# A two-layer transformer kernel: its head rebuilt, the first block in halves, gate rows from column strips, and another order of work

## The chip, the cores and the metric

The kernel runs on one NeuronCore of one Trainium2 chip. The metric is the device time of one execution in microseconds (us); lower is better. Engines are named as the profile names them: PE (TensorE, matrix products), PEld (its weight loads), DVE (VectorE), ACT (ScalarE), POOL (GpSimd) and SP (SyncE, which only issues DMAs and semaphore waits here). A name with a q (SPq, ACTq) is that engine's sequencer issuing a DMA.

## The reference

Input x is 1 × 2048 × 448 in bf16. One condition vector c (1 × 448) gives six modulation rows. Layer A is causal attention with 16 heads of 28 and a window of 256; layer B is a gated MLP that mixes over the sequence.

```python
mod = silu(c) @ w_mod                       # 448 x (6 * 448): sa, ca, ga, sb, cb, gb
h = layernorm(x) * (1 + ca) + sa
q, k, v = split(h @ wqkv)                   # 16 heads of 28
p = softmax(where(0 <= i - j < 256, q k^T / sqrt(28), -1e9))
x = x + ga * ((p v) @ wo)
h = layernorm(x) * (1 + cb) + sb
z1, z2 = split(gelu(h @ w_in))              # 896 columns each
g = w_sp @ layernorm(z2) + b_sp             # over the 2048 rows
x = x + gb * ((z1 * g) @ w_out)
```

## The kernel before

The sequence is cut into 16 tiles of 128 rows (`t` or `j`), four tiles to a block (`tb`). For each block x is normalized (`xn`, tile statistics at L591, normalization at L604 on DVE or L610 on POOL), transposed to `hT` (features on partitions) and modulated with `modT`. Blocks 0 and 1 are transposed by PE (L660) and modulated as they are copied out of PSUM (L672, L674); blocks 2 and 3 by DMA transposes on SP, and then modulated in place (L655). Products with `WQK` (L689) give `qT` and `KT`, four groups of four heads each, and products with `wv` (L742) give `Vaug`, values with a column of ones. `WQK` is made from the staged `wq_st` by a copy that spreads heads of 28 columns over 32 (L583 on ACT, L584 on DVE or POOL).

For each tile j come scores (L818 for the first two tiles, L844 and L853 after them; L853 needs `QBD`, a block-diagonal copy of q which SP spreads by four small DMAs per block, L720), exp on ACT (L805), a mask product on DVE (L860, L880), the products with the values (L887), the division (L901, L903), a DMA transpose, and the output projection (L912) with `wo_g`, which is wo with its columns scaled by the gate `ga` (POOL, L580). Then come the second normalization, a second transposing, w_in products with gelu (L997, L1018), the mixing products (L1041) against the DMA-transposed w_sp (`wspA`, `wspB`), and the final products (L1058) whose sums with x (`fin`, L1068, DVE) SP writes out.

The modulation is made of `sc_sb` (silu of c, on partitions) and `wmod`. For the first layer 32 products of one column write `modT` columns (L528). For the second layer 40 more do (L528, L533), and each gate row is made on all 128 partitions by four products against `sc_rep`, c copied 128 times (L574), and copied to `gg_sb` (L577).

The program is recorded as operations with dependencies. The table `ORDER` lists them: each word has the number of an operation, its engine and its buffers, and every engine runs its operations in that order. `Sched.waits` adds the semaphore waits that the dependencies need, and only those. Durations and landing times in the code serve the making of the table; nothing is computed from them on the chip. PE also runs filling products on the identity matrix (L559), whose results nobody reads.

Loads are issued by SP and ACT. The load of `wv`, the second quarter of x and the rest of `wmod` wait on SP until the first part of `wmod` has landed; the third and fourth quarter of x stand on SP behind the spread of q for block 0.

## Time and profile before

| | us |
|---|---|
| median of 3 runs | 280.66 |
| the three runs | 280.28, 280.66, 281.29 |
| the profiled execution, first to last instruction | 281.0 |
| PE busy in it | 269.3 (96%) |
| DVE busy | 164.3 (58%) |
| ACT busy | 128.5 (46%) |
| POOL busy | 126.1 (45%) |

The profiled execution is one run of the program; its span lies among the times of the three runs. In a row of the windows the first column is the stretch in us from the span's start and its length; then come the busy us and the instruction count of each engine, the granted clock of PE (1.00 is full), the mean busy share of the 16 DMA engines, and GB/s. In a row of the timeline stand start and length in us, engine, line, operation, and in brackets the idle time before it and what ended it. In a row of the chain of waits stand start, length and what ran. A PE product's own length includes its way through the array; where many follow each other, the step from one row to the next tells what each costs.

### The profile page before, as it was taken

The page shows a single profiled execution, that of the slowest core. Times are in us where ns is not written, and L with a number is a line of the kernel's source. Part 1 is how long each engine was busy: PE and PEld are TensorE (multiplying, and loading weights), DVE is VectorE, ACT ScalarE, POOL GpSimd, SP SyncE. Part 2 cuts the span into 40 slices and gives each one's busy share as a digit, 9 for nine tenths or more (in the row PEclk, how much of TensorE's full clock was granted, in tenths as well). Part 3 has the DMA queues.
Part 4 walks back from the last instruction along what each step waited for, and adds up shares of the span by engine and source line. Part 5 has one row for each costly group of instructions (what it writes and reads, how often), then busy time and mean ns, then how long its engine had stood idle before and what let it go on. Part 6 is the DMA issues. An engine that isn't in the chain of part 4 may idle for free.

```text
span 281.0 us, 7380 instructions
## 1 busy us (share of the span) xinstructions
PE 269.3 (96%) x3198; PEld 142.3 (51%) x3222; DVE 164.3 (58%) x355; ACT 128.5 (46%) x151; POOL 126.1 (45%) x200
## 2 busy tenths in 40 slices
PE   6799999799999999999999999999999999999995
PEld 2445556456657777544444444444444444444452
DVE  6347999599899999968898600000243003124443
ACT  4548899789999999866666700000000000000000
POOL 8231177921027989947769503001477101436110
PEclk9789999999999999999999999999999999999999
DMA  6775735343315485693699989910000000000032
GB/s 199 188 261 157 267 58 98 84 55 72 72 23 75 63 96 80 162 103 79 125 181 186 168 181 201 163 36 0 0 2 0 0 0 2 16 16 16 19 98 98
DMA packets 65347, 26.01 MB, mean 93 GB/s; under 512 B 56418, under 2 KB 64227, under 8 KB 65315
## 3 DMA queue, kind: packets, MB, share of 16 engines
q1 hardware_dynamic: 64496, 24.39, 43.6%
q10 hardware_dynamic: 818, 1.15, 1.5%
q8 instruction: 25, 0.41, 0.6%
q14 instruction: 8, 0.06, 0.1%
HBM read 9.01 MB, written 1.84 MB: 39 GB/s over the span
## 4 chain that ended last, share of the span: by engine, by line
PE 80%; POOL 5%; DVE 4%; ACT 4%; issue 3%; DMA 3%; ACTq 0%; POOLq 0%
PE ps L1041 34%; PE ps L997 8%; PE ps L1058 8%; PE ps L1018 8%; PE ps L689 6%; PE ps L887 4%; ACT PW L805 3%; PE ps L912 3%; DMA wmod<-in_w_mod_dram 3%; PE ps L844 2%; PE ps L742 2%; PE ps L853 1%; POOL xn L610 1%; PE ps L729 1%; POOL wo_g L580 1%
## 5 line engine op out<-in xcount | busy, mean ns | idle before, releaser
L805 ACT ACTIVATE PW<-ps 128x2048 bf16<-128x2048 f32 (+1 forms) x56 | 67.8, 1240 | 4.3 <-PE ps L844 2.6
L1048 POOL TENSOR_TENSOR z1T<-tmpg,z1T 128x512 bf16<-128x512 bf16 x28 | 31.7, 1152 | 77.9 <-DVE tmpg L1045 77.9
L1045 DVE TENSOR_TENSOR tmpg<-ps,bsp_bc 128x512 bf16<-128x512 f32 x28 | 19.0, 689 | 79.2 <-PE ps L1041 70.3
L1041 PE MATMUL ps<-wspB,z 128*128 128x512 bf16 x219 | 49.2, 379 | 0.3
L1041 PE MATMUL ps<-wspA,z 128*128 128x512 bf16 x219 | 48.9, 379 | 0.4 <-issue 0.2
L860 DVE TENSOR_TENSOR PT<-PW,mask 128x1024 bf16<-128x1024 bf16 x56 | 39.2, 729 | 0.3 <-ACT PW L805 0.2
L1041 PEld LDWEIGHTS ps<-wspA,z 128*128 128x128 bf16 x224 | 21.8, 98 | 26.6 <-issue 0.4
L1041 PEld LDWEIGHTS ps<-wspB,z 128*128 128x128 bf16 x224 | 21.9, 98 | 26.3
L596 POOL TENSOR_SCALAR ve_all<-mv_all 128x1 f32<-128x1 f32 (+2 forms) x37 | 11.3, 312 | 46.7 <-DVE mv_all L594 45.9
L689 PE MATMUL ps<-hT,WQK 128*128 128x512 bf16 x98 | 25.5, 388 | 2.4 <-POOL hT L655 1.4
L597 POOL TENSOR_TENSOR rs_all<-ve_all,neghalf 128x1 f32<-128x1 f32 (+2 forms) x37 | 25.3, 694 | 1.1
L887 PE MATMUL ps<-Vaug,PT 128*128 128x32 bf16 x496 | 24.4, 177 | 0.5 <-DVE PT L860 0.5
L887 PEld LDWEIGHTS ps<-Vaug,PT 128*128 128x128 bf16 x496 | 21.8, 96 | 4.4 <-DVE o_sb L903 0.9
L997 PE MATMUL ps<-w_in,hT 64*128 64x448 bf16 x224 | 22.7, 349 | 0.2 <-ACT PW L805 0.2
L1018 PE MATMUL ps<-hT,w_in 64*128 64x512 bf16 x196 | 22.3, 376 | 0.0
L1058 PE MATMUL ps<-w_out_g,z1T 128*128 128x448 bf16 x112 | 21.8, 353 | 0.0
L887 PE MATMUL ps<-Vaug,PW 128*128 128x32 bf16 x224 | 20.2, 176 | 0.0
L591 DVE BATCH_NORM_STATS2 st_all<-x_sb 128x6 f32<-128x448 bf16 x32 | 19.2, 610 | 0.4 <-DMA x_sb<-in_A_x_dram 0.4
L610 POOL TENSOR_SCALAR xn<-x_sb,rs_all,ve_all 128x448 bf16<-128x448 bf16 x22 | 18.9, 863 | 0.3
L887 PEld LDWEIGHTS ps<-Vaug,PW 128*128 128x128 bf16 x224 | 17.6, 96 | 1.9
L591 DVE BATCH_NORM_STATS2 st_all<-z 128x6 f32<-128x448 bf16 x32 | 18.1, 602 | 0.2 <-ACT z L1004 0.2
L1004 ACT ACTIVATE z<-ps 128x896 bf16<-128x896 f32 x16 | 14.1, 915 | 8.3 <-PE ps L997 8.2
(100 smaller groups left out, 333.1 us busy)
## 6 DMA issues: line engine op xcount, KB each, us to landing
out_dram<-fin SPq DMA_DIRECT2D x16, 112.0 KB, 1.7
x_sb<-in_A_x_dram SPq DMA_DIRECT2D x3, 448.0 KB, 4.9
wmod<-in_w_mod_dram SPq DMA_DIRECT2D x1, 1344.0 KB, 8.6
w_in<-in_B_w_in_dram SPq DMA_DIRECT2D x1, 1344.0 KB, 8.9
QBD<-qT SPq DMA_DIRECT2D x16, 64.0 KB, 2.0
w_out_g<-in_B_w_out_dram SPq DMA_DIRECT2D x1, 784.0 KB, 5.3
bsp_bc<-in_B_b_sp_dram SPq DMA_DIRECT2D x1, 512.0 KB, 6.8
wmod<-in_w_mod_dram SPq DMA_DIRECT2D x2, 224.0 KB, 6.1
```

Source lines behind the costliest of these rows:

```text
L591: st = [dve(0.62 if True else 0, lambda e, t=t, ci=ci, s=s: e.bn_stats(st_all[:, slot, t, ci, :], s()), deps(t), prio) for ci, s in enumer ...
L597: rs = pool(0.53 + 0.15 * len(tiles), lambda e: e.tensor_tensor(rs_all[:, slot, a:b], ve_all[:, slot, a:b], neghalf[:, 0:b - a], ALU.pow), ...
L610: "pool": (0.9, lambda e: e.tensor_scalar(to[:, h.slot[0], 0:D], x_sb[:, t, :], z, ve, ALU.mult, ALU.add))}, [nm], prio, [h])
L689: mms = [lambda e, h=h, g=g, kc=kc, tb=tb: e.matmul(ps[:, h.slot[0], :], lhsT=WQK[:, kc, 4 * g:4 * g + 4, :].rearrange("p a b -> p (a b)") ...
L805: ex = act(xdur, lambda e, out_ap=out_ap, in_ap=in_ap: e.activation(out_ap(), in_ap(), ACT.Exp, scale=SCALE), [s], v - 8.0 + u, takes, tab ...
L860: return dve(0.70, lambda e: e.tensor_tensor(cols(hp.slot[0] * 2048 + 1024 * k, [[256, 4], [128, 2], [1, 128]]), cols(at_w() + 128 + 192 * ...
L887: fns.append(lambda e, hp=hp, hO=hO, hi=hi, bi=bi, kb=kb, hd=hd, nb=nb, a=at[hi][bi], p_of=p_of: e.matmul(ps[:, hO.slot[0], 32 * hd:32 * h ...
L997: return lambda e, kc, p0, start, stop: e.matmul(ps[:, hs[t % 2].slot[hf], 0:D], lhsT=hT[p0:p0 + 64, kc, t * 128:(t + 1) * 128], rhs=w_in[ ...
L1018: return lambda e, kc, p0, start, stop: e.matmul(ps[:, hs[b // 2].slot[b % 2], :], lhsT=w_in[p0:p0 + 64, kc, ft * 128:(ft + 1) * 128], rhs ...
L1041: m = pe(16 * MMS, [lambda e, h=h, si=si, ft=ft, tb=tb: e.matmul(ps[:, h.slot[0], :], lhsT=z2[:, si, ft * 128:(ft + 1) * 128], rhs=(wspA i ...
L1048: u = pool(1.16, lambda e, ht=ht, ft=ft, tb=tb: e.tensor_tensor(z1T[tb][:, ft, :], tmpg[:, ht.slot[0], :], z1T[tb][:, ft, :], ALU.mult), [ ...
L1058: return [lambda e, ft=ft: e.matmul(ps[:, h.slot[0], 0:D], lhsT=z1T[t // 4][:, ft, (t % 4) * 128:(t % 4 + 1) * 128], rhs=w_out_g[:, ft, :] ...
```

## The change

One line of loads. All loads of the head but that of c are now issued by SP, in the order of need and without waits: two tiles of x, the first 960 columns of w_mod in four pieces of rows, two tiles of x, the q and k columns of wqkv in four pieces, wv, the second quarter of x, the rest of w_mod, the third quarter, wo, the fourth quarter. On SP, before, in the order of the program (`wmod` here is w_mod in SBUF, `wq_st` the staged q and k weights):

```order
L415 DMA x_sb<-in_A_x_dram 128x2x448
L410 DMA wmod<-in_w_mod_dram 128x896
L411 DMA wmod<-in_w_mod_dram 64x896
L410 DMA wq_st<-in_A_wqkv_dram 128x896
L411 DMA wq_st<-in_A_wqkv_dram 64x896
L397 DMA wv<-in_A_wqkv_dram 128x3x448 [waits d_wmAb,d_wmAc,d_wmAa]
L398 DMA wv<-in_A_wqkv_dram 64x448
L404 DMA x_sb<-in_A_x_dram 128x4x448
L397 DMA wmod<-in_w_mod_dram 128x3x1792
L398 DMA wmod<-in_w_mod_dram 64x1792
L720 DMA QBD<-qT 32x2x512 [waits act]
```

and now, further down the same queue, from the second quarter of x on:

```order
L414 DMA x_sb<-in_A_x_dram 128x4x448
L409 DMA wmod<-in_w_mod_dram 128x3x1728
L410 DMA wmod<-in_w_mod_dram 64x1728
L414 DMA x_sb<-in_A_x_dram 128x4x448
L409 DMA wo_g<-in_A_wo_dram 128x3x448
L410 DMA wo_g<-in_A_wo_dram 64x448
L414 DMA x_sb<-in_A_x_dram 128x4x448
L562 DMA modrow<-rows_68 4x448 [waits act]
L564 DMA gg_sb<-modrow 128x448 [waits d_mr0]
L481 DMA_TRANSPOSE hT<-xn 128x4x128 [waits dve]
L481 DMA_TRANSPOSE hT<-xn 128x4x128 [waits pool]
```

The wait for the first part of w_mod is gone, the x quarters stand ahead of everything that waits for a computation, and the spread of q (L686 now) follows the four transposes of block 2.

First block in halves. Block 0 is normalized, transposed, modulated and projected as two halves of 256 rows, and the products of the first half are ordered by row pieces of the weights, as these become ready. The modulation of the first layer is added up over four groups of eight products, one group for each piece of w_mod, and one DVE reduction writes `modT`. On PE the stretch from the first transposes to the first dense products was (L660 transposes, L528 modulation, L559 filling, L689 projections):

```order
L660 MATMUL ps<-ident,xn 128x128 x4
L528 MATMUL ps<-sc_sb,wmod 128x1 x12
L528 MATMUL ps<-sc_sb,wmod 64x1 x4
L528 MATMUL ps<-sc_sb,wmod 128x1 x12
L528 MATMUL ps<-sc_sb,wmod 64x1 x4
L660 MATMUL ps<-ident,xn 128x128 x12
L559 MATMUL ps<-ident 128x512 x4
L689 MATMUL ps<-hT,WQK 128x512
L559 MATMUL ps<-ident 128x512 x2
L689 MATMUL ps<-hT,WQK 128x512 x23
```

and is now, around the second half's transposes (L627 transposes, L548 filling, L646 projections of a half, L672 values of block 0):

```order
L548 MATMUL ps<-ident 128x512
L548 MATMUL ps<-ident 128x128
L627 MATMUL ps<-ident,xn 128x128 x4
L548 MATMUL ps<-ident 128x128 x3
L627 MATMUL ps<-ident,xn 128x128 x4
L548 MATMUL ps<-ident 128x128 x2
L646 MATMUL ps<-hT,WQK 128x256
L548 MATMUL ps<-ident 128x512
L672 MATMUL ps<-wv,hT 128x448 x4
L646 MATMUL ps<-hT,WQK 128x256 x16
```

The modulation products now stand ahead of the transposes, the filling is spread among the products in pieces of 512 and 128 columns, and the projections go by 256 columns.

Gates as column strips. The four rows ga, gb, sb, cb are made at once on four strips of 32 output columns of the array (16 products of 448 columns), copied to `rows4`, written to DRAM, and read back: the gates broadcast to 128 partitions, the second layer's modulation gathered into `modT`. The one that is added to 1 gets it from a row of ones in `wmod`.

Also: the products with the values use 29 columns instead of 32, so that three columns of `Vaug` need no zeros; tile 1 is written out in two halves of columns, the second as the last of the program; some zeroing moves between engines; and of the 32 normalizations DVE now does 24 instead of 10. On DVE, before, from a normalization of block 1 to the third mask product (L880, L860 masks, L577 gate rows):

```order
L604 TENSOR_SCALAR xn<-x_sb,mv_all,rs_all 128x448 [waits pool]
L577 COPY gg_sb<-ps 128x448 [waits pe]
L880 TENSOR_TENSOR PT<-PT,mask_60 128x4x128 [waits act]
L604 TENSOR_SCALAR xn<-x_sb,mv_all,rs_all 128x448 [waits pool]
L880 TENSOR_TENSOR PT<-PT,mask_60 128x4x128
L577 COPY gg_sb<-ps 128x448 [waits pe]
L674 TENSOR_SCALAR hT<-ps,modT 128x512 [waits pe]
L674 TENSOR_SCALAR hT<-ps,modT 128x512 [waits dve]
L880 TENSOR_TENSOR PT<-PT,mask_60 128x4x128 [waits act]
```

and now, up to the second mask product (L578 statistics, L677 and L790 values to `Vaug`, L591 normalization, L903 masks):

```order
L730 TENSOR_SCALAR hT<-ps,modT 128x512 [waits act]
L578 BN_STATS st_all<-x_sb 128x6 [waits d_x3]
L677 CAST Vaug<-ps 128x16x28 [waits pe]
L591 TENSOR_SCALAR xn<-x_sb,mv_all,rs_all 128x448 [waits pool]
L578 BN_STATS st_all<-x_sb 128x6
L790 CAST Vaug<-ps 128x16x28 [waits pe]
L903 TENSOR_TENSOR PT<-PW,mask_60 128x1024
L591 TENSOR_SCALAR xn<-x_sb,mv_all,rs_all 128x448 [waits pool]
L903 TENSOR_TENSOR PT<-PW,mask_60 128x1024
```

The statistics of the third and fourth quarter of x, which wait for their loads, stand ahead of the first mask. Between the first and the last mask on DVE there are 14 statistics instead of 20, and 10 normalizations instead of 1.

The core of the diff (of the table `ORDER` one line of each):

```diff
-2.a 21.v 30.g 1.s 22.v 23.v 24.v 33.g 34.g 0.a 4.s 31.g 3.a 28.g 25.v 5.s 32.g 6.a 26.v 35.g 50.v 51.p.0 7.s 40.a 8.s 52.p.1 36.g 107.v 53.p.2 109.v
...
-    t_wmA = load3("d_wmA", wmod, w_mod, slice(0, 2 * D), -98.95, 7.75, 4.5, 6.7)
-    t_wq = load3("d_wq", wq_st, A_wqkv, slice(0, 2 * D), -98.9, 9.6, 8.4, 9.4)
-    t_wv = load2("d_wv", "sp", 0.35, wv, ALL, A_wqkv, slice(2 * D, 3 * D), [t_wmA], -95.5)
+    t_wmA = [chunk("d_wmA", "sp", wmod, w_mod, kc, slice(0, 2 * D + 64), -98.95 + 0.001 * kc, LAND_M[kc], 0.23) for kc in range(DC)]
+    t_x0.append(load("d_x01", "sp", 0.25, lambda e: e.dma_start(x_sb[:, 2:4, :], x_d[:, 2:4, :]), prio=-98.92, land=7.8))
+    t_wq = [chunk("d_wq", "sp", wq_st, A_wqkv, kc, slice(0, 2 * D), -98.9 + 0.001 * kc, LAND_Q[kc], 0.23) for kc in range(DC)]
+    t_wv = load2("d_wv", "sp", 0.35, wv, ALL, A_wqkv, slice(2 * D, 3 * D), (), -95.5)
...
+    t_rows = pe(0.8, [lambda e, v=v, i=i, kc=kc: e.matmul(
+        ps[32 * i:32 * i + 32, hR.slot[0], 0:D], lhsT=sc_rep[:, kc, :], rhs=wmod[:, kc, v * D:(v + 1) * D],
+        start=(kc == 0), stop=(kc == DC - 1), tile_position=(0, 32 * i)) for kc in range(DC) for i, v in enumerate((2, 5, 3, 4))],
+        [t_wmA, t_wmB, t_screp, t_p2], -15.0, [hR], "cols32")
...
+    t_gg = [load("d_mg%d" % gi, "sp", 0.1, lambda e, gi=gi: e.dma_start(gg_sb[:, gi, :], modrow[gi:gi + 1, 0:D].broadcast_to([128, D])), [t_rowd[0]], -14.8) for gi in range(2)]
+    t_mc = load("d_mc", "sp", 0.05, lambda e: e.dma_start(modT[:, 8:16], modrow[2:4, :].rearrange("v (c p) -> p (v c)", p=128), allow_slow_non_contiguous=True), [t_rowd], -14.7)
...
+    for half in range(2):
...
+            if half == 0:
+                for kc in range(DC):
+                    m = pe(0.109, parts[kc], [evs[kc], t_wqk[kc], m], v + 1 + kc * 0.1 + 0.01 * g, [] if kc else [h])
+            else:
+                m = pe(0.436, parts, [evs, t_wqk], v + 1 + 0.1 * g, [h])
...
-                            ps[:, hO.slot[0], 32 * hd:32 * hd + 32], lhsT=p_of(a), rhs=Vaug[:, kb, hd, :],
+                            ps[:, hO.slot[0], 32 * hd:32 * hd + DH + 1], lhsT=p_of(a), rhs=Vaug[:, kb, hd, 0:DH + 1],
...
+            if t == SPLIT:
+                for c0 in (0, 224):
```

416 lines of the change are left out of this document (234 added, 182 removed).

## The prediction

> **What bounds the kernel now.** I read the windows of busy time first, then the chain of waits, the timelines of the head, the groups by form, and the queue of SP.
>
> ```profile
> core 0: us, PE busy (x) PEld busy (x) DVE busy (x) ACT busy (x) POOL busy (x), PEclk, DMA share, GB/s
> 2.00:9.00 7.00, 5.40 (x20) 1.86 (x20) 5.20 (x16) 3.71 (x6) 5.43 (x12) 1.00 0.95 278
> 9.00:11.00 2.00, 1.31 (x32) 1.27 (x32) 0.00 (x0) 1.00 (x2) 0.00 (x0) 0.74 0.29 60
> 11.00:14.00 3.00, 3.00 (x20) 1.94 (x19) 1.65 (x7) 2.45 (x3) 1.15 (x1) 0.50 0.83 207
> 14.00:18.00 4.00, 3.78 (x13) 1.55 (x13) 2.44 (x6) 1.14 (x2) 0.00 (x0) 0.65 1.03 398
> 18.00:22.00 4.00, 4.00 (x21) 1.86 (x20) 0.50 (x5) 2.76 (x6) 3.21 (x8) 1.00 0.22 65
> 26.12:112.15 86.03, 82.65 (x2035) 54.51 (x2047) 80.57 (x169) 79.85 (x82) 47.21 (x71) 1.00 0.48 94
> 49.00:56.00 7.00, 5.29 (x103) 2.79 (x104) 3.76 (x9) 5.59 (x7) 6.91 (x12) 1.00 0.38 82
> 112.00:160.00 48.00, 47.70 (x501) 23.13 (x485) 41.70 (x103) 32.71 (x47) 35.75 (x73) 1.00 0.83 141
> 160.00:278.00 118.00, 117.37 (x552) 54.67 (x560) 27.60 (x43) 2.06 (x4) 31.72 (x28) 1.00 0.25 50
> ```
>
> From 112 us on TensorE alone sets the pace: it is busy for 165.07 of 166 us. From 26.12 (the first mask product) to 112.15 (the end of the last mask product on the chain) three engines are nearly full: TensorE 82.65, VectorE 80.57 and ScalarE 79.85 of 86.03 us. So a head that ends earlier is worth only what all three can use. The one hole is at 49 to 56 us, where VectorE and TensorE both have room. In the head the transfers stall (60 GB/s from 9 to 11 us, 65 from 18 to 22) and TensorE's granted clock stands at 0.50.
>
> ```profile
> 7.52 0.40 PE L660 MATMUL ps<-ident,xn 128*128 128x128 bf16 x4
> 9.69 1.47 PE L528 MATMUL ps<-sc_sb,wmod 128*128 128x1 bf16 x32 [1.78 <-DMA wmod<-in_w_mod_dram]
> 11.12 0.40 DVE L584 COPY WQK<-wq_st 128x896 bf16<-128x896 bf16 x1 [2.65 <-DMA wq_st<-in_A_wqkv_dram]
> 9.50 0.95 ACT L583 ACTIVATE WQK<-wq_st 128x896 bf16<-128x896 bf16 x1 [1.77 <-DMA wq_st<-in_A_wqkv_dram]
> 12.23 0.78 ACT L672 ACTIVATE hT<-ps,modT 128x512 bf16<-128x512 bf16 x1 [0.34 <-PE ps L660]
> 9.66 0.38 SPq L397 DMA_DIRECT2D wv<-in_A_wqkv_dram  x1
> 23.82 0.59 SPq L404 DMA_DIRECT2D x_sb<-in_A_x_dram  x1
> 25.02 0.49 SPq L404 DMA_DIRECT2D x_sb<-in_A_x_dram  x1
> 15.55 5.63 PE ps L689 x23
> 53.64 0.87 PE ps L689 x4
> ```
>
> The modulation products wait 1.78 us for wmod. SP issues wv only at 9.66, after wmod has landed, and the third and fourth quarter of x at 23.82 and 25.02, behind the copies of q. The dense projection products stand on the chain from 15.55.
>
> **The change, part by part.** *Loads.* In the new line on SP 2072 KB (2.12 MB) stand up to the last piece of wq: x twice 224, wmod 840, wq 784. At the 278 GB/s of the row from 2 to 9 us, counted from 2.0, the last byte arrives at 9.6. In the old run nearly as many bytes were through at 10 us and the last WQK copies started at 11.12, so I add 1.1 us: wq at 10.7, and wmod (1064 KB with the x piece ahead of it) at some 7 instead of 9.69. Fifteen issues of about 0.5 us leave SP before it has to wait for anything. What is late next is a chain of copies on ScalarE: WQK, two hT pieces, WQK, two hT pieces of the second half. With the second WQK copy from 10.7 on, that is 10.7 + 0.95 + 2 × 0.45 = 12.6 us (0.45 is an estimate for 256 columns from the 0.78 of 512). The first half's own products and V can go a little earlier; I take 12.5. *Term 1: dense products from 15.5 to 12.5, −3.0 us.*
>
> *Clock and fillers.* The 23 products lasted 5.63 us; by the later four in 0.87 they need 5.0. *Term 2: −0.6*, if the fillers hold the clock. The fillers themselves run where TensorE would wait for wmod, xn or WQK and cost nothing there; if one of these came early, a wide one would hold it up by 0.2. The halves make 64 products of 256 columns from 32 of 512, the same columns: 0.
>
> [...]
>
> ```profile
> 24.00 0.76 PE ps L574 x4
> 25.93 0.88 PE ps L574 x4
> 28.55 0.57 PE L528 MATMUL ps<-sc_sb,wmod 128*128 128x1 bf16 x13
> 29.67 0.17 PE L533 MATMUL ps<-sc_sb,wmod 128*64 128x1 bf16 x1
> 47.16 0.55 PE L844 MATMUL ps<-qT,KT 32*128 32x128 bf16 x36
> ```
>
> *Gates.* Gone are eight products of 448 columns (0.76 + 0.88) and the 40 single-column products from 28.55 to 29.84 (1.3): 2.9 us. In come 16 products of 448 columns in strips of 32. No row shows column strips. Upper bound: one after another, 16 × 0.19 = 3.0. Lower bound: four at once, 0.8. The nearest row is that of the row strips, 2560 columns in 0.55 us where one after another they need 1.07, so strips do overlap. I take 1.1. *Term 3: −1.8.*
>
> [...]
>
> The strips wait for the rest of wmod: 4.53 MB in the line, by 278 GB/s at 18.3 + 1.1, by the 398 of the row 14 to 18 us for what follows wq at 15.7 + 1.1. All later products queue behind them, and TensorE gets there near 18.7: 0 to 0.7 lost, *term 4: +0.4*. The way of the gates through DRAM (write, broadcasts, a gather of single elements) is two landings long, some 6 us, and ends near 27.
>
> ```profile
> 44.83 1.42 POOL wo_g L580
> 50.67 1.52 POOL hT L655
> 52.54 0.81 PE ps L689 x3
> 53.34 0.29 PE ps L887 x12
> 278.15 0.62 DVE fin L1068
> ```
>
> The first scaling of wo by its gate stood at 44.83, so 17 us cover that way; without them the output projections would wait for it. In the hole at 49 to 56 us TensorE waits for hT of the third x quarter, which GpSimd scales until 52.19. That quarter now lands between 18 and 21 us instead of behind an issue at 23.82, and its transposes should be done well ahead. TensorE can get back at most 7.00 − 5.29 = 1.7; *term 5: −1.5.* The last output is cut in two, so the VectorE sum behind the last product has 224 columns instead of 448: *term 6: −0.3* of 0.62. The PV products with 29 columns for 32 take nothing away: twelve last 0.29 us, 24 ns each, where 32 columns at 0.87 us for 2048 are 14 ns, so something else sets them.
>
> TensorE's own sum, with +0.8 for waits of the new order (between 0 and the 3.4 us it idles in the row 26 to 112): −3.0 − 0.6 − 1.8 + 0.4 − 1.5 − 0.3 + 0.8 = **−6.0 us.** The other two engines decide how much of it stays.
>
> ```profile
> L860 DVE TENSOR_TENSOR PT<-PW,mask x56: 626/679/1616, 37.5 to 115.9; 128x1024 bf16<-128x1024 bf16 x56
> L860 DVE TENSOR_TENSOR PT<-PW,mask 128x1024 bf16<-128x1024 bf16 x56 | 39.2, 729 | 0.3 <-ACT PW L805 0.2
> L591 DVE BATCH_NORM_STATS2 st_all<-x_sb 128x6 f32<-128x448 bf16 x32 | 19.2, 610 | 0.4 <-DMA x_sb<-in_A_x_dram 0.4
> L604 DVE TENSOR_SCALAR xn<-x_sb,mv_all,rs_all 128x448 bf16<-128x448 bf16 x10 | 4.1, 431 | 3.5 <-DMA hT<-xn 2.1 <-POOL rs_all L597 0.8 <-POOL ve_all L608 0.6
> L747 DVE CAST Vaug<-ps 128x448 bf16<-128x448 f32 x7 | 4.3, 615 | 4.0 <-PE ps L742 4.0
> L674 DVE TENSOR_SCALAR hT<-ps,modT 128x512 bf16<-128x512 bf16 x6 | 3.2, 539 | 0.9 <-PE ps L660 0.8
> 26.12 0.42 DVE L880 TENSOR_TENSOR PT<-PT,mask 128x512 bf16<-128x512 bf16 x1
> 23.61 1.02 ACT L805 ACTIVATE PT<-ps 128x1024 bf16<-128x1024 f32 x1
> ```
>
> *VectorE.* Its instructions follow one another some 0.08 us sooner than they last. Ahead of the first mask the new order has ten x statistics (0.53), three V casts (0.54), five half-wide casts (0.3), four normalizations (0.35) and small ones: 11.6 us from 12.1 on, with waits for two x quarters and a V product on the way. The first mask stays near 26. Between first and last mask there are six statistics fewer (20 to 14, −3.2), four hT pieces from PSUM fewer (−1.8), small ones −1.2, but nine normalizations more (1 to 10, +3.2) and casts, hT pieces and copies for +1.9: −1.1. The normalizations leave GpSimd, and masks of 679 ns reached 1616 where GpSimd ran beside them; the mean of 729 makes that 56 × 0.05 = 2.8 us, of which I take half, −1.4. Of VectorE's 5.5 idle us 3.2 lie at 49 to 56; I take back 2.0. Together **−4.5** at the attention's end. *ScalarE.* Its first exp comes after three V groups and 27 products of 256 columns, 2.3 + 2.9 us from 12.5, one score group and the loading of the table: near 18.8 for 23.61, with the same 80 us of work: −4.8, and 0.2 back for the strips' wait, **−4.6**.
>
> The least of the three is −4.5, and the tail's −0.3 comes on top: 281.0 − 4.8 = **276.2** for the profiled execution. Its span of 281.0 stands 0.3 above the median of 280.66 (280.28 to 281.29), which makes 275.9; I say **276.0**.
>
> **The rivals.** (B) *TensorE's gain arrives whole.* Terms 1, 2, 3, 5 and 6 without new waits are −7.2: 281.0 − 7.2 − 0.3 = 273.5. For it: GpSimd loses fourteen normalizations (22 to 8), so VectorE could be quicker than I count. Against: VectorE, 94% busy, would have to reach 98%. (C) *VectorE becomes the bound* and keeps its idle share and its mean mask: only −1.1 and −0.3 are left, 279.3. For it: its first mask doesn't move. (F) *The clock falls again.* Between the first transposes and the last WQK copy TensorE has little but short fillers; a gap like the 1.8 us would halve the clock for some 4.5 us of dense products: 276.0 + 2.2 = 278.2. [...] (D) *The head doesn't do what it says:* the copies on ScalarE queue, the dense products start when they did, and a new hole opens for the old one, 280.4. (E) *Slower.* On VectorE the first statistics of the last x quarter stand ahead of two V casts and of every mask, 2.5 us with what lies between. 5.85 MB lie in the line up to that quarter. At 278 and then 398 GB/s it lands near 20, at 278 throughout near 24. At the 207 of the row 11 to 14 us it lands at 2.0 + 28.3 + 1.1 = 31.4, the first mask comes at 33.9, 7.8 late, and with −1.1, −1.4, −2.0 and −0.3 against it the time is 281.0 + 3.0 − 0.3 = 283.7. It decides from a landing at 28.4 on. For it: many short rows are in the line. Against: 278 and 398 came before and after.
>
> **How the numbers follow.** The forecast has 0.44, with its own range 274.2 to 278.0; B 0.17, C 0.17, F 0.07, D 0.06, E 0.09. The range of 8 in 10, 272.8 to 279.6, leaves out E, D and the low end of B. This kernel's measurement can tell 0.3% (0.84 us) from no change. Faster: forecast, B, C and F, 0.85; same: D, 0.06; slower: E, 0.09.
>
> **What would show it.** Right: no gap in the transfers from 9 to 11 us; the first modulation products before 7 us; a granted clock of 1.00 through the head; dense products from 12 to 13; the first exp before 20 and the first mask near 26; TensorE busy for over 6.5 of the 7 us at 49 to 56; a last VectorE sum near 0.4 us. Wrong: strips of 0.19 us each; a first mask past 28; masks still at a mean of 729 ns; TensorE waiting for the spread copies of q, which now stand behind four transposes on SP. Most of all: if the time between first exp and last mask grows as much as the head shrinks.

## The result and the profile after

The changed kernel takes 282.78 us (median of 20 runs, 281.84 to 284.26). The kernel before took 280.75 us in the 20 runs beside them. The ratio is 1.0080, with a 95% interval of 1.0061 to 1.0100: slower by 0.8%, where 276.0 us was predicted. The profiled span is 282.1 us for 281.0.

One thing has to be known about the numbers of the kernel before. Of its 121 runs beside the experiments, 51 had a mean granted clock of 0.999 or 1.0 and a median span of 278.2 us, 56 had 0.992 to 0.994 and 279.5 us, and 14 had 0.982 to 0.988 and 281.4 us; the profiled execution of the prediction (281.0 us, clock 0.988) belongs to the last kind. All 20 runs of the changed kernel had a clock of 0.999 or 1.0, with a median span of 281.05 us. So it is some 2.8 us behind the kernel before at full clock. In every timed run the time is longer than the span, by 1.67 to 1.83 us; 1.75 is used below.

The windows of the changed kernel, with the columns of the prediction's first block:

```profile
core 0: us, PE busy (x) PEld busy (x) DVE busy (x) ACT busy (x) POOL busy (x), PEclk, DMA share, GB/s
2.00:9.00 7.00, 5.34 (x52) 2.83 (x53) 4.55 (x11) 2.93 (x6) 1.44 (x4) 1.00 0.98 303
9.00:11.00 2.00, 2.00 (x13) 1.28 (x12) 1.26 (x6) 0.97 (x2) 0.43 (x2) 1.00 1.11 264
11.00:14.00 3.00, 3.00 (x18) 1.58 (x17) 2.23 (x8) 1.84 (x3) 2.23 (x4) 1.00 1.06 396
14.00:18.00 4.00, 4.00 (x41) 3.01 (x39) 2.33 (x7) 2.07 (x3) 0.00 (x0) 1.00 1.06 292
49.00:56.00 7.00, 6.89 (x166) 4.43 (x165) 6.69 (x14) 6.17 (x6) 0.00 (x0) 1.00 0.67 84
63.00:70.00 7.00, 5.74 (x137) 3.67 (x135) 6.19 (x15) 6.22 (x8) 3.59 (x7) 1.00 0.25 56
98.00:105.00 7.00, 6.03 (x172) 4.03 (x164) 6.28 (x13) 5.73 (x6) 2.79 (x5) 1.00 0.69 113
```

The loads do what was foreseen: no gap at 9 to 11 us (264 GB/s for 60), and the old hole at 49 to 56 us is closed (6.89 of 7 us). But two new ones are open at 63 to 70 and 98 to 105 (5.74 and 6.03 us busy, where the kernel before had 6.95 and 7.00). The surprise is in the head. The clock column says 1.00 throughout, and TensorE is busy, yet look at what it does and how long that takes. The timeline of TensorE in the changed kernel (start, duration, line, shapes, count, and in brackets the idle time before):

```profile
5.81 0.35 PE L537 MATMUL ps<-sc_sb,wmod 128*128 128x1 bf16 x8 [1.10 <-ACT sc_sb L525]
...
9.40 1.06 PE L548 MATMUL ps<-ident 128*128 128x512 bf16 x2
10.25 0.63 PE L627 MATMUL ps<-ident,xn 128*128 128x128 bf16 x4
10.68 2.74 PE L548 MATMUL ps<-ident 128*128 128x512 bf16 x8
13.25 0.27 PE L646 MATMUL ps<-hT,WQK 128*128 128x256 bf16 x1
...
16.00 0.92 PE L672 MATMUL ps<-wv,hT 128*128 128x448 bf16 x4
```

Eight fillers (six of 512 columns, two of 128) stand from 10.68 to 13.25, the first five of them 0.43 us apart. At full rate 512 columns take 0.22 us (23 of them take 5.13 us further down), so this is half rate, though the column reads full clock. The first projection product waits behind them until 13.25, and dense work begins only at 16.00, where the profile before had it at 15.34. The following rows are of VectorE and ScalarE, out of the timeline of all engines of the changed kernel: the modulation's sum, the first pieces of hT, the copy of WQK1, the first exp and the first mask.

```profile
10.15 0.16 DVE L542 TENSOR_REDUCE modT<-ps 128x8 f32<-128x32 f32 x1
...
11.00 0.73 DVE L639 TENSOR_SCALAR hT<-ps,modT 128x256 bf16<-128x256 bf16 x2 [0.61 <-PE ps L627]
...
12.50 0.60 DVE L571 COPY WQK<-wq_st 128x896 bf16<-128x896 bf16 x1 [0.77 <-issue]
...
21.71 1.28 ACT L848 ACT_TABLE_LOAD   x1
...
23.00 1.02 ACT L848 ACTIVATE PT<-ps 128x1024 bf16<-128x1024 f32 x1
...
30.40 0.68 DVE L903 TENSOR_TENSOR PT<-PW,mask 128x1024 bf16<-128x1024 bf16 x1
```

The first pieces of hT were done at 11.4 us, so the fillers and not the data held the products. On the chain of waits, too, TensorE stands without a break from 6.87 to 20.85 us. The first exp comes at 23.00 (18.8 predicted) and the first mask at 30.40 (26 predicted).

### The profile page after: what moved, and what is told of

Its sections match the earlier page's. It is cut to its first block, busy times and chain, and to the rows that moved or that the text cites. A ratio compares the mean times of both kernels' runs of the same rounds, so it can differ in the third digit from the quotient of the medians.

```text
span 282.1 us, 7443 instructions
## 1 busy us (share of the span) xinstructions
PE 269.5 (96%) x3231; PEld 145.5 (52%) x3254; DVE 166.3 (59%) x373; ACT 131.4 (47%) x159; POOL 108.6 (38%) x181
## 4 chain that ended last, share of the span: by engine, by line
PE 74%; DVE 18%; DMA 5%; issue 1%; POOL 1%; SPq 0%; POOLq 0%
PE ps L1085 34%; PE ps L1061 7%; PE ps L1102 7%; DVE PT L903 7%; PE ps L1040 7%; DMA hT<-o_sb 3%; PE ps L743 3%; PE ps L548 2%; PE ps L930 2%; DVE st_all L578 2%; DVE o_sb L946 2%; PE ps L887 2%; PE ps L955 2%; DMA wmod<-in_w_mod_dram 2%; DVE x_sb L960 2%; DVE xn L591 1%
## 5 line engine op out<-in xcount | busy, mean ns | idle before, releaser
L903 DVE TENSOR_TENSOR PT<-PW,mask 128x1024 bf16<-128x1024 bf16 x56 | 38.0, 702 | 0.2 <-ACT PW L848 0.2
L583 POOL TENSOR_SCALAR ve_all<-mv_all 128x1 f32<-128x1 f32 (+2 forms) x37 | 10.6, 290 | 57.2 <-DVE mv_all L581 57.1
L584 POOL TENSOR_TENSOR rs_all<-ve_all,neghalf 128x1 f32<-128x1 f32 (+2 forms) x37 | 24.4, 667 | 1.5
L930 PE MATMUL ps<-Vaug,PT 128*128 128x29 bf16 x496 | 23.8, 176 | 1.0 <-DVE o_sb L946 0.4
L1102 PE MATMUL ps<-w_out_g,z1T 128*128 128x448 bf16 x105 | 20.7, 352 | 0.0
L930 PE MATMUL ps<-Vaug,PW 128*128 128x29 bf16 x224 | 20.2, 175 | 0.0
L578 DVE BATCH_NORM_STATS2 st_all<-z 128x6 f32<-128x448 bf16 x32 | 18.4, 603 | 2.4 <-ACT z L1047 2.4
L578 DVE BATCH_NORM_STATS2 st_all<-x_sb 128x6 f32<-128x448 bf16 x32 | 19.0, 611 | 1.0 <-DMA x_sb<-in_A_x_dram 1.0
L743 PE MATMUL ps<-hT,WQK 128*128 128x512 bf16 x67 | 17.1, 379 | 1.9 <-DVE KT L661 0.8
L1069 ACT ACTIVATE z1T<-ps 128x512 bf16<-128x512 f32 x28 | 14.7, 610 | 5.0 <-PE ps L1061 4.9
```

Source lines behind the costliest of these rows:

```text
L578: st = [dve(0.62 if True else 0, lambda e, t=t, ci=ci, s=s: e.bn_stats(st_all[:, slot, t, ci, :], s()), deps(t), prio) for ci, s in enumer ...
L584: rs = pool(0.53 + 0.15 * len(tiles), lambda e: e.tensor_tensor(rs_all[:, slot, a:b], ve_all[:, slot, a:b], neghalf[:, 0:b - a], ALU.pow), ...
L743: m = pe(4 * MMS, [lambda e, h=h, g=g, kc=kc, tb=tb: e.matmul(ps[:, h.slot[0], :], lhsT=WQK[:, kc, 4 * g:4 * g + 4, :].rearrange("p a b -> ...
L903: return dve(0.70, lambda e: e.tensor_tensor(cols(hp.slot[0] * 2048 + 1024 * k, [[256, 4], [128, 2], [1, 128]]), cols(at_w() + 128 + 192 * ...
L930: fns.append(lambda e, hp=hp, hO=hO, hi=hi, bi=bi, kb=kb, hd=hd, nb=nb, a=at[hi][bi], p_of=p_of: e.matmul(ps[:, hO.slot[0], 32 * hd:32 * h ...
L1102: return [lambda e, ft=ft: e.matmul(ps[:, h.slot[0], 0:D], lhsT=z1T[t // 4][:, ft, (t % 4) * 128:(t % 4 + 1) * 128], rhs=w_out_g[:, ft, :] ...
```

## The experiments

Every experiment ran beside the kernel before, on the same chip. In their profiles a line number can stand one or two off, because the table `ORDER` is longer or shorter. Edits are shown as words of that table; `N.p.0` is operation N on TensorE with buffer 0, v is VectorE, a ScalarE, g GpSimd, s SP.

**First group: the head, or the amount of work on VectorE?** Three theories are tested. A: TensorE starts at half rate and its slow fillers hold the head up. B: VectorE's amount of work sets the end. C: the rate has nothing to do with how long TensorE has been busy.

`e1_warm`: six wide fillers more, right after the first seven.

```diff
- 97.p.0 98.p.0 99.p.0 52.p.1
+ 97.p.0 98.p.0 99.p.0 76.p.0 77.p.0 78.p.0 79.p.0 80.p.0 81.p.0 52.p.1
```

> The changed kernel with one edit: six more filler products of 512 columns (about 0.43 us each as the changed kernel's trace has them) ahead of the first modulation product, so that TensorE is busy from 2.5 us without the 1.10 us hole at 4.7 to 5.8. Theory A (TensorE's first 13 us run at half rate because it was never busy long enough, and its line of fillers then holds everything behind it up): the fillers after 7 us take 0.22 instead of 0.43 us, the first projection product starts near 11 instead of 13.25, the dense products near 14 instead of 16, first exponential near 21 instead of 23.0; the end follows by 1.5 to 2.5 us, ratio to the kernel before 0.999 to 1.003 where the changed kernel has 1.008. Theory B (VectorE's amount of work from 21 to 119 us sets the end, the head does not): the head starts earlier, but the end stays, ratio 1.006 to 1.010. Theory C (the rate is not a matter of how long TensorE was busy): the fillers stay at 0.43 us, the modulation products start about 1 us later, and the time grows by 0.5 to 1 us, ratio 1.010 to 1.012.

`e2_fewer`: no filler after the first seven (61 to 75 and 100 to 120 taken out of the table).

> The changed kernel without the 36 filler products that stand after the first modulation product (the first seven stay). Theory A: the transposes and the first projection products are no longer held up and start near 11.5 us instead of 13.25, but at half rate (about 0.22 us per 256 columns) for some 4 us, so that the dense stretch reaches the first scores at 21 to 22 us as before; ratio 1.004 to 1.010, and the half rate shows in the duration of the projection products. Theory C (the fillers only stand in the way, the rate does not depend on them): products at full rate from the start, first scores near 18.5, ratio 0.996 to 1.000. Theory B: ratio 1.006 to 1.010.

`e3_pool`: eight normalizations from VectorE to GpSimd.

```diff
- 355.v.0 ... 349.v.1 ... 351.v.2 ... 353.v.3 ... 415.v.0 ... 442.v.1 ... 558.v.0 ... 587.v.1
+ 355.g.0 ... 349.g.1 ... 351.g.2 ... 353.g.3 ... 415.g.0 ... 442.g.1 ... 558.g.0 ... 587.g.1
```

> The changed kernel with eight normalizations of 0.39 us that VectorE does between 47 and 101 us given to GpSimd (0.71 to 1.26 us each there), nothing else moved. Theory B (VectorE's amount of work sets the end): 8 x 0.39 = 3.1 us less in its line, the end 2 to 3 us earlier, ratio 0.997 to 1.001. Theory A (the late head and an order that no longer fits are the cause, VectorE is full only because it is waited on in turn): within 0.7 us of the changed kernel, ratio 1.005 to 1.010.

`e4_head`: the fillers of `e1_warm`, and another order in the head.

```diff
- 145.p 194.v ... 132.a 30.v ... 195.v 56.v 197.v 146.v ... 147.a 149.v ... 152.p 47.g 75.p.0
+ 145.p 56.v 146.v 149.v 194.v ... 132.a 147.a ... 195.v 197.v 30.v ... 152.p 75.p.0 ... 249.g.2 47.g
```

> The six more fillers, and beside them the order of the head: the sum over the modulation products and the two casts that it frees on VectorE ahead of the statistics of tile 3, the memset of wv behind those statistics, and GpSimd's clear of QBD (0.95 us at 11.7) behind the normalization of the second block. Theory A: the modulation is there near 9.3 instead of 10.3 and the first products near 10.5, the dense products near 13, first exponential near 20; ratio 0.993 to 0.999. Theory B: ratio 1.005 to 1.010, although the head is earlier. If the fillers alone matter, the same as with them alone.

Measured against the kernel before: `e1_warm` 1.0052 (1.0020 to 1.0084), `e2_fewer` 1.0038 (1.0012 to 1.0063), `e3_pool` 1.0081 (1.0055 to 1.0107), `e4_head` 1.0123 (1.0080 to 1.0167). TensorE's timeline in `e1_warm`:

```profile
2.58 4.64 PE L548 MATMUL ps<-ident 128*128 128x512 bf16 x13
...
9.66 1.57 PE L548 MATMUL ps<-ident 128*128 128x512 bf16 x8
11.07 0.27 PE L646 MATMUL ps<-hT,WQK 128*128 128x256 bf16 x1
...
13.09 0.28 PE L646 MATMUL ps<-hT,WQK 128*128 128x256 bf16 x1 [0.54 <-DVE WQK L571]
...
14.53 0.92 PE L672 MATMUL ps<-wv,hT 128*128 128x448 bf16 x4
```

The thirteen fillers before the first products (ten of 512 columns) go at half rate, and then the same eight fillers take 1.57 us instead of 2.74, and the first projection product starts at 11.07. Theory C falls: full rate came at about 7.0 us here and at 13.0 in the changed kernel, so it depends on how TensorE worked before. The timeline of `e2_fewer`, which has almost nothing but its own products:

```profile
10.41 1.04 PE L644 MATMUL ps<-hT,WQK 128*128 128x256 bf16 x4 [1.44 <-DVE hT L637]
12.57 0.39 PE L644 MATMUL ps<-hT,WQK 128*128 128x256 bf16 x1 [1.13 <-DVE WQK L569]
...
13.93 1.70 PE L670 MATMUL ps<-wv,hT 128*128 128x448 bf16 x4
15.43 1.78 PE L644 MATMUL ps<-hT,WQK 128*128 128x256 bf16 x8
```

Now the products themselves run at half rate: eight of 256 columns start 0.21 us apart from 15.43 (0.11 is full rate), and the spacing falls to 0.11 at 16.9, 4.3 us after the last pause, which ended at 12.57. Fillers held the products up, and without them the products themselves run at half rate until 16.9 us; both kernels reach the dense stretch near 14.

In the two profiled executions most of the head's shift arrives: in `e1_warm` dense work starts 1.47 us earlier than in the changed kernel, the sum of the last tile comes 1.37 us earlier, the end 1.1 us; in `e2_fewer` 2.07 us at the dense start become 1.7 at the end. Over all runs it is less: the median spans are 280.35 and 280.25 us for 281.05, so 0.7 and 0.8 us. The ratio of `e1_warm` misses theory A's 0.999 to 1.003, and its interval overlaps what theory B gave (1.006 to 1.010); that of `e2_fewer` comes out at the edge of theory A's 1.004 to 1.010. So the traces show theory A's mechanism, and in the times about half of the shift of the head is seen. Theory B is decided by `e3_pool`. The window from 28 to 120 us, the changed kernel first and then `e3_pool`:

```profile
28.00:120.00 92.00, 87.03 (x2041) 56.22 (x2051) 86.51 (x187) 83.08 (x86) 40.65 (x68) 1.00 0.49 95
```

```profile
28.00:120.00 92.00, 86.04 (x2032) 55.92 (x2044) 83.03 (x174) 81.86 (x84) 46.00 (x74) 1.00 0.48 94
```

VectorE lost 3.5 us of its 86.5 (the eight normalizations at 0.39 us are 3.1 of them), and the time stayed (1.0081 for 1.0080). Its high share does not make it the bound. `e4_head` was a miss: 0.993 to 0.999 was expected. The modulation's sum came at 9.09 instead of 10.15, but the fillers still stood ahead of the first products (10.98), and the statistics of tile 3, pushed back, made the transposes of the second half wait: dense work at 15.31, 0.8 us later than in `e1_warm`.

**Second group: local repairs.**

`e5_holes`: `e1_warm`, and moves against the five largest holes of its trace.

```diff
- 243.v.0 216.p.6 247.v.1 214.p.1 209.v 249.g.2 217.v 121.p.0 215.v 245.v.3
+ 243.v.0 209.v 216.p.6 247.v.1 214.p.1 249.g.2 121.p.0 215.v 245.v.3 217.v
- 290.v ... 254.a 286.v 190.p.6 252.v ... 287.v 255.v
+ 290.v 252.v ... 254.a 255.v 286.v 190.p.6 ... 287.v
- 295.v.3 185.p.0 ... 189.v
+ 185.p.0 ... 189.v 295.v.3
- 522.p.1 ... 547.p 595.v 619.p.0        - 667.p.0 ... 668.v 713.p 720.p
+ ... 547.p 595.v 619.p.0 522.p.1        + ... 713.p 720.p 667.p.0 668.v
```

> The changed kernel with the six more fillers of e1_warm, and eight instructions moved by a few places: on VectorE four casts and modulations for which TensorE was seen to wait (op 209, 252, 255, 189) ahead of normalizations and statistics nobody waits for yet, on TensorE the attention's output products of tiles 4 and 9 two places later, behind work that is ready. In e1_warm's trace TensorE is idle 0.38, 0.33, 0.84, 0.71 and 1.07 us there, 3.3 us in sum. Theory A (the order no longer fits the time at which things are there, each hole is local): the five holes close without new ones, 2.5 to 3.3 us earlier than e1_warm, ratio 0.993 to 0.997. Theory B (VectorE is full, what it does earlier for one it does later for another): half or less comes out, the holes turn up at other places, ratio 1.000 to 1.005.

`e6_copies`: `e1_warm` with a head in which ScalarE copies WQK0, 1 and 2, VectorE makes all four hT pieces of the first half, GpSimd's clear comes later, and the transposes of the second half stand ahead of the products with WQK2; 16 fillers fewer stand between.

```diff
- 132.a ... 147.a 149.v ... 148.a ... 133.v 134.a ... 151.p ... 201.p.5.3 135.v ... 203.p ... 152.p 47.g
+ 56.v 196.v 194.v ... 132.a 199.g 146.v 147.v 148.v 149.v ... 133.a ... 134.a ... 151.p 166.p 171.p 161.p 202.v.3 201.p.5.3 203.p ... 135.v ... 152.p 172.p 162.p 167.p
```

> The six more fillers, and the head in another order: ScalarE makes three of the four padded copies of WQK and VectorE all four modulated transposes of the first half (VectorE's copy of WQK1 took 1.77 us from the end of the work before it to its own end in e1_warm, for 0.4 us of work, while GpSimd worked), the modulation's sum ahead of the statistics of the second half, GpSimd's clear of QBD later, the transposes of the second half ahead of the products that wait for WQK2, and 16 fillers fewer between. Theory A (the head's start is set by these three queues and passes on whole): the first projection products near 10.7, dense from 12.5 instead of 14.5, first scores near 18, the end 1.5 to 2 us earlier than e1_warm, ratio 0.997 to 1.000. Theory D (what TensorE gains is lost again before the first scores, since x1 and the casts behind it set them): first scores within 0.5 us of e1_warm's 19.7, ratio 1.003 to 1.006.

`e7_both`: both edits. `e8_table`: both, and one exp of a single column on ScalarE at 5 us.

> The two edits before together. If both gains are real and at separate places they add: 4 to 5 us earlier than e1_warm, ratio 0.987 to 0.992. If VectorE takes over (theory B), no better than the better of the two, 0.996 to 1.002.

> The kernel of the two edits, and one more: an exponential of one column on ScalarE at 5 us, where it is idle, so that the table load of 1.3 us that stands ahead of the first exponential (21.7 us in the changed kernel) is done by then. First exponential 1.3 us earlier than in e7_both. If ScalarE's first exponential is on the path, 0.5 to 1.3 us earlier than e7_both at the end; as I read the trace ScalarE waits for scores right after, so 0 to 0.5 us.

Measured: `e5_holes` 1.0084 (1.0053 to 1.0114), `e6_copies` 1.0027 (0.9999 to 1.0055), `e7_both` 1.0101 (1.0058 to 1.0145), `e8_table` 1.0091 (1.0057 to 1.0124). The groups of TensorE between 20 and 120 us (count, busy time, mean ns, then the idle time before them and what ended it), first `e1_warm`, then `e5_holes`:

```profile
L930 PE MATMUL ps<-Vaug,PT 128*128 128x29 bf16 x496 | 23.7, 176 | 1.0 <-DVE o_sb L946 0.4 <-DVE mv_all L581 0.4 <-DVE PT L903 0.2
...
L743 PE MATMUL ps<-hT,WQK 128*128 128x512 bf16 x67 | 17.1, 379 | 1.9 <-DVE KT L661 0.8 <-DVE hT L730 0.3 <-issue 0.2
...
L955 PE MATMUL ps<-wo_g,hT 128*128 128x448 bf16 x56 | 12.6, 353 | 1.8 <-DMA hT<-o_sb 1.8
```

```profile
L930 PE MATMUL ps<-Vaug,PT 128*128 128x29 bf16 x496 | 23.8, 176 | 2.3 <-DVE o_sb L946 1.2 <-DVE PT L903 0.6 <-DVE mv_all L581 0.4
...
L743 PE MATMUL ps<-hT,WQK 128*128 128x512 bf16 x67 | 17.3, 379 | 2.5 <-DVE Vaug L790 1.1 <-DVE KT L661 0.6 <-DVE hT L730 0.2
...
L955 PE MATMUL ps<-wo_g,hT 128*128 128x448 bf16 x56 | 12.6, 353 | 0.3 <-DMA hT<-o_sb 0.3
```

The projections' wait for the transposes falls from 1.8 to 0.3 us, and 1.9 us come back elsewhere: a cast moved back makes the projections wait 1.1 us, the value products wait 2.3 us for 1.0. From 15.5 to 122 us TensorE idles 5.9 us in `e1_warm` and 6.0 in `e5_holes`. A repair by hand at five places only moved the idle time, and the ratio, 1.0084, is worse than either theory gave (0.993 to 0.997, 1.000 to 1.005).

`e6_copies` is the other case. Its head, rows of ScalarE, VectorE and TensorE out of the timeline of all engines:

```profile
9.40 1.79 ACT L569 ACTIVATE WQK<-wq_st 128x896 bf16<-128x896 bf16 x2 [0.17 <-DMA wq_st<-in_A_wqkv_dram]
...
9.84 1.33 DVE L638 TENSOR_SCALAR hT<-ps,modT 128x256 bf16<-128x256 bf16 x4
...
11.37 0.60 PE L645 MATMUL ps<-hT,WQK 128*128 128x256 bf16 x4
...
12.37 1.04 PE L645 MATMUL ps<-hT,WQK 128*128 128x256 bf16 x8
```

Dense work starts at 12.37, which is the 12.5 of the prediction, and the profiled span is 278.1 us: 3.6 us of head give 4.0 us at the end. But that execution is the fastest of 12. The median span is 279.2 us, 1.85 us below that of the changed kernel, so again about half arrives. Over its 12 runs `e6_copies` is level with the kernel before, between its two theories (0.997 to 1.000, 1.003 to 1.006), although its first scores, at 17.89 us, come as early as theory A had it. `e7_both` is slower than both of its theories (0.987 to 0.992, 0.996 to 1.002) with a dense start at 12.84; why the moved words cost so much there is not shown. The early table load of `e8_table` is worth 0.7 us in the trace from 49 us on, less than the runs can tell.

**Third group: what was the kernel before really like?**

`e9_cover`: the kernel before, with four filler groups in the 1.78 us in which its TensorE stood still.

```diff
- 123.p.1 9.s
+ 123.p.1 60.p.4 61.p.5 62.p.4 63.p.5 9.s
```

> The kernel before with one edit: four more filler groups (eight products of 512 columns, 1.7 us at full rate) between its first transposes and the modulation products, where TensorE stood idle for 1.78 us in the profiled execution and the granted clock fell to 0.50 right after. In the 47 timed runs of the kernel before that came with the earlier experiments, 19 had a mean clock of 0.999 or 1.0 with spans mostly near 277.9 us, 20 one of 0.992 to 0.994 near 279.5, and the rest 0.982 to 0.988 near 280.7, as in the profiled one (281.0, 0.988). Theory A (the idle stretch lets the clock fall, for a different time in each execution, and the profile that the prediction rested on was one of the longest): a clock of 1.0 in all runs, span 277.5 to 278.5, ratio to the kernel before 0.990 to 0.995, first dense product near 13.5 and first exponential near 21 where the profile before had 15.5 and 23.6. Then the changed kernel's head, at 16.0 and 23.0, was never ahead of it. Theory F (the clock falls for another reason): clocks as mixed as before, ratio 0.998 to 1.002.

`e10_table` is `e6_copies` with the early table load, `e11_cover_table` is `e9_cover` with it.

> e6_copies with the exponential of one column at 5 us, so that the table is loaded while ScalarE is idle. From e7_both to e8_table this moved everything from 49 us on 0.7 us earlier in the trace, so 0.5 to 0.9 us earlier than e6_copies: ratio 0.998 to 1.001 where that had 1.0027, span 277.0 to 277.8. If ScalarE is not on the path in this head: the same as e6_copies.

> The kernel before with the covered gap of e9_cover and the early table load of e8_table. In its profile the load stands at 22.32 to 23.60, right ahead of the first exponential at 23.61, whose scores were there at 23.02; so that exponential can go 0.6 us earlier, and the ones behind it. Ratio 0.002 to 0.004 below e9_cover's. If the first exponential is not on the path: the same as e9_cover.

Measured: `e9_cover` 0.9991 (0.9966 to 1.0016), `e10_table` 1.0018 (0.9990 to 1.0046), `e11_cover_table` 1.0007 (0.9977 to 1.0036). In the timeline of all engines of `e9_cover` the dense stretch of TensorE and the first exp:

```profile
13.37 5.13 PE L689 MATMUL ps<-hT,WQK 128*128 128x512 bf16 x23
...
21.14 1.02 ACT L805 ACTIVATE PT<-ps 128x1024 bf16<-128x1024 f32 x1
```

In the profile of the prediction the same stretch is

```profile
15.34 5.84 PE L689 MATMUL ps<-hT,WQK 128*128 128x512 bf16 x23
```

So `e9_cover` shows the head of the old kernel with its clock held (the column reads 1.00 from 2 to 18 us): 13.37 and 21.14 us, where the profile of the prediction had 15.34 and 23.61, and the changed kernel has 16.00 and 23.00. All sums of the attention come 2.6 us earlier than in that profile, the end 2.0 us. The changed head is 2.6 us behind the old one at the dense start and 1.9 at the first exp, not level with it. The cover raises the share of runs at full clock from 51 of 121 to 9 of 12 (37 of 48 in the four kernels `e9_cover`, `e11_cover_table`, `e14_strips_late` and `e15_scalar`) and does not make it whole: the other three still had 0.994. The median moved by less than can be told. Theory A (the pause lets the clock fall) holds for the profile (0.50 from 11 to 14 us behind the pause, 1.00 there without it); its claim that all runs would be at full clock fell, and so did its ratio of 0.990 to 0.995: 0.9991 is what the other theory gave (0.998 to 1.002). The table load did not show in either kernel's time.

**Fourth group: the strips alone.**

`e12_strips`: `e9_cover` with one part of the change, the four rows from column strips and their way through DRAM, in the old order. `e13_strips_table`: with the early table load. Names stand for the new operations.

```diff
- 95.p.0 324.a.0 177.v.2 96.v ... 97.p.0 98.v ... 92.p.1 ... 94.v 93.v
+ strips.p.0 ... rows.v write0.s write1.s ga.s gb.s columns.s addone.g
```

> The kernel before with the covered gap of e9_cover and one part of the change alone: the two gates and the second pair of modulation vectors as 16 products in four column strips with the way through DRAM, in the order of the kernel before (strips where the first gate's products stood, four small transfers in a stretch in which SP issues nothing). On TensorE 0.94 us stand for 1.7 us of gate products and 1.3 us of single-column products, on VectorE one copy of 0.63 us for two of 0.65 and two small ones. Theory A (the old order was full of work on three engines from 26 us on, so a part can give back most of what it saves while its order is kept): attention ends 1.0 to 2.0 us earlier than in e9_cover's trace (last reciprocal of the sums at 115.5 us), ratio 0.992 to 0.996 where e9_cover has 0.9991. Theory B (the three engines share the bound, TensorE's 2 us there come out as idle time): 0 to 0.7 us earlier, ratio 0.997 to 1.000.

> The same, and the early load of the table of e11_cover_table, which moved the attention 0.5 us earlier in the trace (115.5 to 115.0) though not the median. By theory A 0.5 us earlier than e12_strips, ratio 0.990 to 0.995, the fastest of the kernels here; by theory B as e12_strips.

Measured: 1.0190 (1.0130 to 1.0250) and 1.0203 (1.0144 to 1.0262), far slower than either theory (0.990 to 1.000). GpSimd's timeline in `e12_strips`:

```profile
36.75 0.24 POOL L581 TENSOR_SCALAR modT<-modT 128x4 f32<-128x4 f32 x1 [14.69 <-DMA modT<-modrow]
```

The small addition waited 14.69 us for the columns to come back from DRAM, and the third block's normalizations stood behind it; then SP was late with the copies of q, and TensorE stood 5.95 us at 52.3. That is one word in a wrong place. `e14_strips_late` moves it behind the scalings of wo.

> e12_strips with one word moved: in its trace GpSimd stood 14.7 us, from 22.1 to 36.8, waiting for the second modulation pair to come back from DRAM, with the third block's normalizations queued behind; the addition that waits now stands behind the scalings of wo, 20 us later and long before its first user. So the copies of q and the third block come when they did in e9_cover, and the experiment says what e12_strips should have said. Theory A (a part keeps its saving in the old order): attention's end 1 to 2 us earlier than e9_cover's 115.5, ratio 0.992 to 0.996. Theory B (TensorE's 2 us are idled away): 0 to 0.7 us earlier, ratio 0.997 to 1.001.

Measured: 1.0007 (0.9984 to 1.0029), where `e9_cover` has 0.9991. The saving is real on TensorE and does not arrive; the sum of the last tile comes at 115.64 us, in `e9_cover` at 115.50. TensorE in `e14_strips_late`, then in `e9_cover`:

```profile
21.06 0.94 PE L571 MATMUL ps<-wmod,sc_rep 128*32 128x448 bf16 x16
...
25.31 0.38 PE L855 MATMUL ps<-QBD,KT 128*128 128x512 bf16 x1
27.33 0.40 PE L820 MATMUL ps<-qT,KT 32*128 32x128 bf16 x16 [1.64 <-ACT PT L807]
```

```profile
23.23 0.93 PE L574 MATMUL ps<-wmod,sc_rep 128*128 128x448 bf16 x4
...
25.53 0.38 PE L853 MATMUL ps<-QBD,KT 128*128 128x512 bf16 x1
...
27.49 0.40 PE L818 MATMUL ps<-qT,KT 32*128 32x128 bf16 x16 [0.28 <-ACT PT L805]
```

The next scores start at 27.33 and 27.49 us: they wait for ScalarE's exps to empty their banks, and the single-column products had filled most of that wait (0.28 us is left of it in `e9_cover`, 1.64 here). `e15_scalar` takes the table load and the clear of QBD (1.06 us) out from ahead of those exps.

```diff
- 43.a ... 158.a 331.a.1 ... 47.a
+ 43.a exp.a ... 47.a 158.a 331.a.1
```

> e14_strips_late, in whose trace TensorE then stands 1.64 us at 27.33 waiting for an exponential, with two pieces of ScalarE's line moved into its idle time: the table load (1.28 us at 19.46) to 5 us, and the clear of QBD (1.06 us at 24.25, ahead of the two exponentials waited for) to 21.8, where ScalarE waits 1.13 us for a product. If ScalarE's line is what idles the saving of the strips away (theory B's mechanism): the gap shrinks from 1.64 to below 0.8 us, the attention ends 0.8 to 1.8 us earlier than in e14_strips_late, ratio 0.994 to 0.998. If something else sets the pace from there on (VectorE, or all three in turn): the gap shrinks, the end does not move by more than 0.4 us, ratio 0.999 to 1.002.

Measured: 0.9990 (0.9966 to 1.0015). The wait went from 1.64 to 1.32 us only, and the attention ran 0.6 us earlier until 100 us and 0.2 us at its last tile. ScalarE's other work was not what set it: in this trace the scores at 26.71 us wait for two exps of 2.08 us together, and these for the scores before them (0.51 us). None of these kernels is measurably faster than the kernel before.

## Why the prediction was wrong

**The base.** The prediction said that the profiled span "stands 0.3 above the median of 280.66". A span and a time are not the same measure: with the 1.75 us between them that execution would have a time of 282.75, 2.1 above the median, and the 276.2 forecast for it are a time of some 278.0 and not 275.9 (both are estimates from the 1.75). It was an execution with an unusually bad head: only 14 of the 121 runs have so low a clock. Much of what the terms for the head took back was not lost in a usual run. By `e9_cover` 2.0 us of the forecast gain belonged to that execution.

**Term 1 (dense products from 15.5 to 12.5).** This is the step that failed. The chain of copies on ScalarE was followed correctly: `e6_copies`, with much the same chain and the queues in another order, reaches 12.37. What failed is the sentence that the fillers "cost nothing" because they run where TensorE would wait. They ran at half rate to 13.0 us here, and in an in-order queue eight fillers stood ahead of products that were ready 1.8 us sooner; the prediction's price for a filler in the way was 0.2. From 13.25 to 16.00 TensorE has no idle time either: 1.6 of these 2.75 us are fillers again. With the fillers quicker or gone the next limit shows: a product waits 0.54 us in `e1_warm` and 1.13 in `e2_fewer` for VectorE's copy of WQK, with the second half's transposes behind it. So rival D came in its outcome, dense products as late as before and new holes for the old one, though by the fillers and not by copies that queue on ScalarE.

**Term 2 (−0.6).** The clock column is 1.00, and 23 full products do take 5.13 us at full clock, as the row of `e9_cover` has it. That is the old kernel, so none of it belongs to the change. Rival F, a clock that falls again, did not come: the column stays at 1.00, and TensorE, at 0.43 us for 512 columns up to 12.8 us, had not yet reached full rate.

**Term 3 (strips, −1.8).** The size was right: 16 products in 0.94 us, and the row of the changed kernel says the same.

```profile
L555 PE MATMUL ps<-wmod,sc_rep 128*32 128x448 bf16 x16 | 0.9, 355 | 0.4 <-DVE qT L661 0.4
```

By the prediction's 3.0 us for one after another that is 3.2 times as fast with four strips.

What it is worth was not right. `e14_strips_late` shows the saved time turned into idle time at the next scores. The prediction named the limit itself ("worth only what all three can use") and then carried the term into TensorE's sum.

**Term 4 (+0.4)** has its size by luck: the strips waited 0.4 us, but for a qT cast and not for the rest of w_mod. **Term 5 (−1.5)**: the hole at 49 to 56 closed as said. **Term 6 (−0.3)**: the last sum takes 0.39 us for 0.62, which makes 0.2.

```profile
L1113 DVE TENSOR_TENSOR fin<-ps,x_sb 128x224 bf16<-128x224 f32 x2 | 0.8, 386 | 0.0
```

**The +0.8 for new waits.** From 15.5 to 122 us TensorE idles 5.8 us in the changed kernel and 3.7 in the old one. These 2.1 and the 1.4 of the closed hole went into new waits: of those that the view of waits names, 2.5 us are for VectorE, 1.6 for transposes of o_sb and 0.5 for exps. So the term was 3.5 and not 0.8.

**VectorE and ScalarE.** The first mask came at 30.4 instead of 26, since its line starts from the second half's hT (15.8 us for 12.1). The row at 26.12 that the prediction calls the first mask is the second; the first stands at 25.48 in the same view. The first exp came 4.2 us late for the same reason, and 3.5 of these are the dense start. The mean mask fell by the half that was taken, from 729 to 702 ns. The sign of being wrong that the prediction put above all others came: from the first exp to the end of the last mask it takes 95.1 us for 93.0, 2.1 more, while the first exp comes 0.6 us earlier. Rival E, slower, ended on the right side by luck: the statistics of the last x quarter stood where it said, but the quarter was there by 27.4 us, before the 28.4 from which E decides, and nothing waited for it. Rival C falls by `e3_pool`, and rival B by `e14_strips_late`: neither VectorE's amount of work nor TensorE's own sum sets the end.

**How much of the miss is the head.** The table has the dense start and the span (us) of all kernels but `e12_strips` and `e13_strips_table`, in which the wait for DRAM stands in the attention. The dense start is that of the row shown above or of its counterpart. Dense start, span and their difference are of the one profiled execution; the last column is the median span of all runs:

| kernel | dense start | span | difference | median span |
|---|---|---|---|---|
| before, as profiled | 15.34 | 281.0 | 265.7 | 279.1 |
| `e9_cover` | 13.37 | 279.0 | 265.6 | 278.7 |
| `e11_cover_table` | 12.95 | 277.9 | 265.0 | 278.75 |
| `e14_strips_late` | 13.19 | 279.2 | 266.0 | 279.3 |
| `e15_scalar` | 12.90 | 278.5 | 265.6 | 278.6 |
| changed | 16.00 | 282.1 | 266.1 | 281.05 |
| `e3_pool` | 15.80 | 283.0 | 267.2 | 281.15 |
| `e4_head` | 15.31 | 283.3 | 268.0 | 282.2 |
| `e1_warm` | 14.53 | 281.0 | 266.5 | 280.35 |
| `e5_holes` | 14.27 | 281.8 | 267.5 | 280.6 |
| `e2_fewer` | 13.93 | 280.4 | 266.5 | 280.25 |
| `e7_both` | 12.84 | 281.5 | 268.7 | 280.9 |
| `e8_table` | 12.73 | 280.7 | 268.0 | 280.8 |
| `e6_copies` | 12.37 | 278.1 | 265.7 | 279.2 |
| `e10_table` | 12.36 | 279.3 | 266.9 | 278.85 |

What stands behind the dense start takes 265.0 to 266.0 us in the old order, and 265.7 to 268.7 in the new one. The late head is one part of the miss. Where it is as early as predicted, in `e6_copies` and `e10_table`, the kernels take 280.91 and 280.56 us for the 282.78 of the changed one. By these medians 3.6 us of head are worth 1.9 and 2.2 us, by the ratios to the kernel before 1.5 and 1.7. The two times are still 4.6 to 4.9 us above the forecast. Some 2.0 of that is the base, and the other 2.6 to 3.0 are gains behind the head that did not arrive. Why the attention keeps its length, or grows, while TensorE's work shrinks is shown at one place (the scores and exps at 25 to 27 us). For the rest of it, that three nearly full engines wait for one another in turn is the reading that the failed repairs leave, and it was not proved.

## What to carry over

Look at the clock and the span of several executions before you take terms from one profile, and compare spans with spans; the same holds for the profiles of the experiments, of which one was the fastest of its 12 runs and another the slowest. A stretch in which three engines were each some 90% busy gave nothing back here for work saved on VectorE (`e3_pool`) or TensorE (`e14_strips_late`), while about half of a shift of its start came out at the end; so move the start, and check in the timeline that what fills the wait (fillers, clears, statistics) does not stand ahead of the work it was to wait for. After a change of order, read each queue at the place where one word waits for a transfer.
